# Emptying attention's last blocks in three steps between output matmuls, and moving two zero loads to GpSimd's queue

## The chip, the core and the metric

The kernel runs on one core of one Trainium2 chip. The metric is the device time of one execution in microseconds. The kernel before takes 1247.27 us (median of three runs, 1247.18 to 1247.7).

Engine names: PE is the tensor engine's matmuls, PEld its weight loads, DVE the vector engine, ACT the scalar engine, POOL is GpSimd, SP the sync engine. SPq, ACTq and POOLq are the queues from which those engines issue transfers. PSUM is the memory that takes the results of matmuls. An issue holds its queue (or, on GpSimd, the engine) for the time that the profile shows for it; a transfer lands when its data have arrived.

## The reference, cut to what matters

Two independent parts share one output tensor. Part A is a state space layer of 1024 states over 2048 steps. Part B is attention with memory, in 64 segments of 32 tokens plus 8 memory rows, with 32 heads of 128, followed by an output projection:

```python
for s in range(n_seg):
    xs = x[:, s * seg_len:(s + 1) * seg_len, :].copy()
    h = jnp.concatenate([mem, xs], axis=1)
    q = jnp.einsum('btd,dhe->bhte', h, Wq)      # k and v likewise
    scores = jnp.einsum('bhqe,bhke->bhqk', q, k) * scale
    scores = jnp.where(mask[None, None], scores, -1000000000.0)
    p = _softmax(scores, axis=-1)
    o = jnp.einsum('bhqk,bhke->bhqe', p, v)
    o = jnp.einsum('bhte,hed->btd', o, Wo)
    mem = o[:, :M, :].copy()
    outs.append(o[:, M:, :])
...
return jnp.concatenate([a, b], axis=-1)
```

The kernel computes all segments at once with a guess of the memory rows, checks the guess at the end, and has a slow path.

## The kernel before

The order of the program is: part A with the V projection of part B; then attention, in which head pairs (16 of them, `HP`) are projected to q and k while the pair before goes through scores and softmax; then the output projection. PE is given its work in small steps by Python generators. `proj` yields after each projection group, `attention` after each pair of block groups (11 per head pair, `NU`), `outproj_first` after every four output matmuls.

```python
def load_v(self, hp):
    if hp < HP:
        k = self.k
        vt = self.vts[hp % 2]                    # [128, 22, 272] bf16, two buffers
        if hp < 2:                               # the rows past 99 are zeroed once per buffer
            z = self.vx[0][T + 32:T + 32 + 128 - GW, 0:2 * EW].unsqueeze(1).to_broadcast([128 - GW, NG, 2 * EW])
            k.tc.keep_in_program_order(k.SP.dma_start(vt[GW:128, :, :], z))
        hb, cs = ...
        k.tc.keep_in_program_order(k.SP.dma_start(vt[0:GX, :, :], self.vx[hb].rearrange("(g p) n -> p g n", p=GX)[:, :, cs]))
        k.SP.dma_start(vt[GX:GW, :, :], self.vt[hb].rearrange("(g j) n -> j g n", j=3)[:, :, cs])
        self.vtile[hp] = vt
```

Here `GX` is 96, `GW` is 99 and `NG` is 22. So a zero load writes partitions 99 to 127, that is 29 of them, with 22 rows of 544 bytes each: 638 rows, 347,072 bytes (339 KB of 1024).

```python
def att_front(self, hp, u):
    ...                                          # four scores matmuls into PSUM
    k.S.activation(e[:], s[...], ACT.Exp, ...)   # ACT: exponential
    k.G.tensor_tensor(m[...], e[:], mask[...], ALU.mult)   # POOL: times the mask
    return [(hp, 4 * u + b, m, b) for b in range(4)]       # four pending blocks

def att_back(self, blocks):                      # up to three blocks: values, 1/sum, scale
    ...
    for i, (_, b, m, j) in enumerate(blocks):
        PE.matmul(o[:, i, 0:EV], m[:, j * GP:j * GP + 128], vt[:, b // 2, ...], start=True, stop=True)
    V.reciprocal(r, o[0:GW, 0:n, E])
    V.tensor_tensor(self.ob[:, b0:b0 + n, :], o[...], r..., ALU.mult)
    ...                                          # after the last block: stores of ob

def attention(self):
    pend = []

    def back(keep):
        while len(pend) > keep:
            n = min(3, 2 * NG - pend[0][1])
            self.att_back([pend.pop(0) for _ in range(n)])
    for hp in range(HP):
        for u in range(NU):
            if u == 2:
                self.load_v(hp + 1)
            pend += self.att_front(hp, u)
            back(8)
            yield hp, u
    back(0)
    yield HP, 0
```

The loop that drives it. From the moment that the projections run out (in head pair 15), each yield is followed by one step of the output projection:

```python
for n, (hp, u) in enumerate(at):
    if n == 12:
        k.SP.dma_start(wo0[:], b.Wo[:, :, 0:512])          # 4 MB
    ...
    while done < want:
        next(pr)                                           # projection steps
        done += 1
    if done == 18 * HP:
        ...
        next(first)                                        # four output matmuls
```

Two tiles share memory across the border between part A and attention: one of the two q tiles of attention lies where a buffer of part A's output (`a_ot`) was. Its zeroing on DVE therefore waits until part A's last store has landed.

## Time and profile before

| | before |
|---|---|
| span of the profiled run | 1245.6 us |
| PE busy | 1234.4 us, 99% |
| share of PE in the chain that ended last | 98% |
| PE idle in the stretch 480 to 1000 us | 0 |
| PE waits for the mask product | 0.20, 0.26 and 0.43 us, at 1009 to 1016 us |

The first part of the page of the kernel before (busy time, share of the span, number of instructions):

```profile
span 1245.6 us, 20120 instructions
PE 1234.4 (99%) x8270; PEld 662.3 (53%) x8342; DVE 668.0 (54%) x1250; ACT 263.5 (21%) x631; POOL 275.8 (22%) x407
```

PE is the limit. The list of waits of PE between 1000 us and the end has one line: who waited, for whom, the total, how often, and the longest.

```profile
PE psO L64 <- POOL b_m L644: 0.9, 3, 0.4
```

The timeline of the kernel before, where attention ends (start, length, engine, line, operation; in brackets the idle time of that engine and what ended it):

```profile
1014.21 0.34 PE L64 MATMUL psS<-b_q,b_k 128*128 128x99 bf16 x4
...
1014.55 1.03 PE L64 MATMUL psP<-t,b_wv 128*128 128x512 bf16 x4
...
1015.31 0.87 POOL L644 TENSOR_TENSOR b_m<-b_e,maskB 99x396 bf16<-99x396 bf16 x1 [0.34 <-ACT b_e L641]
1015.42 0.39 PE L64 MATMUL psO<-b_v,b_m 128*128 128x129 bf16 x4
...
1016.24 0.29 PE L64 MATMUL psO<-b_v,b_m 128*128 128x129 bf16 x2 [0.43 <-POOL b_m L644]
1016.37 0.28 PE L64 MATMUL psR<-b_v,b_m 128*128 128x129 bf16 x2
```

The last scores are followed by four output matmuls and then by all eight pending blocks.

GpSimd and DVE, before:

```profile
476.89 0.10 DVE L568 MEMSET b_q<- 128x50 bf16 x1 [0.54 <-DMA out_dram<-a_ot]
...
489.75 0.88 POOL L644 TENSOR_TENSOR b_m<-b_e,maskB 99x396 bf16<-99x396 bf16 x1 [0.92 <-ACT b_e L641]
493.16 0.87 POOL L644 TENSOR_TENSOR b_m<-b_e,maskB 99x396 bf16<-99x396 bf16 x1 [2.54 <-ACT b_e L641]
```

The mask products come every few microseconds, and PE reads the third of them (493.16 us) at 494.37 us.

### The profile page before, as it was taken

The numbers are of one execution on the slowest core, as the hardware profiler recorded it, in microseconds if no ns is written. First come the engines' busy times: TensorE is split into PE (matmuls) and PEld (weight loads), VectorE is DVE, ScalarE is ACT, GpSimd is POOL, SyncE is SP. The second block draws the span as 40 slices with busy tenths as digits, with TensorE's granted clock in tenths as the row PEclk, the third lists the DMA queues.
The fourth block names the chain that finished last, engine by engine and source line by source line (L and its number), as shares of the span: only waits on it lengthen the run. The fifth ranks groups of instructions, "written<-read, shape, count | busy, mean of one in ns | idle before, by whom it ended". The sixth has DMA issues, their size and how long they took to land.

```text
span 1245.6 us, 20120 instructions
## 1 busy us (share of the span) xinstructions
PE 1234.4 (99%) x8270; PEld 662.3 (53%) x8342; DVE 668.0 (54%) x1250; ACT 263.5 (21%) x631; POOL 275.8 (22%) x407
## 2 busy tenths in 40 slices
PE   9999999999999999999999999999999999999998
PEld 5444444444455555556666656555665554446444
DVE  4688899998711124666666666666666641001000
ACT  5344444443310000211112111111211110000000
POOL 4111331212332321322222222222222220000000
PEclk9999999999999999999999999999999999999999
DMA  9965444554898834664454544545473289407000
GB/s 245 272 192 148 131 132 128 144 156 107 241 323 247 251 116 95 192 167 123 95 144 108 144 108 114 138 92 133 96 155 95 61 223 220 110 18 153 17 17 27
DMA packets 316022, 176.83 MB, mean 142 GB/s; under 512 B 138650, under 2 KB 301326, under 8 KB 315926
## 3 DMA queue, kind: packets, MB, share of 16 engines
q1 hardware_dynamic: 293830, 147.95, 48.1%
q10 hardware_dynamic: 21072, 24.38, 5.9%
q0 software_dynamic: 1024, 3.17, 0.7%
q8 instruction: 66, 1.08, 0.4%
q14 instruction: 30, 0.25, 0.1%
HBM read 89.14 MB, written 53.17 MB: 114 GB/s over the span
## 4 chain that ended last, share of the span: by engine, by line
PE 98%; DMA 1%; issue 0%; ACT 0%; POOL 0%; DVE 0%; SPq 0%; ACTq 0%
PE psP L64 82%; PE psU L64 9%; PE psS L64 3%; PE psO L64 2%; PE psR L64 2%; DMA wo<-in_B_Wo_dram 1%; DMA b_xr<-in_B_x_dram 0%; ACT b_xe L89 0%; POOL b_m L644 0%; DVE b_ost L91 0%; SPq L64 0%; ACT b_e L641 0%; ACTq L89 0%
## 5 line engine op out<-in xcount | busy, mean ns | idle before, releaser
L64 PE MATMUL psP<-b_xe,b_wq 128*128 128x480 bf16 (+1 forms) x1280 | 247.7, 343 | 0.1
L64 PE MATMUL psP<-b_xe,b_wk 128*128 128x480 bf16 (+1 forms) x1280 | 247.7, 343 | 0.0
L64 PE MATMUL psP<-b_wv,b_xe 128*128 128x512 bf16 (+2 forms) x1033 | 223.4, 372 | 1.0 <-ACT b_xe L89 0.2
L644 POOL TENSOR_TENSOR b_m<-b_e,maskB 99x396 bf16<-99x396 bf16 x160 | 139.8, 874 | 334.0 <-ACT b_e L641 334.0
L641 ACT ACTIVATE b_e<-psS 99x396 bf16<-99x396 f32 x176 | 88.2, 501 | 532.2 <-PE psS L64 527.9
L64 PEld LDWEIGHTS <-b_wk 128*128 128x128 bf16 x1280 | 119.4, 98 | 94.2
L64 PEld LDWEIGHTS <-b_wq 128*128 128x128 bf16 x1280 | 118.7, 98 | 87.7
L64 PEld LDWEIGHTS <-b_xe 128*128 128x128 bf16 x1056 | 101.8, 98 | 119.1 <-ACT b_xe L89 0.4
L91 DVE CAST b_k<-psP 128x480 bf16<-128x480 f32 (+1 forms) x192 | 97.5, 529 | 101.1 <-PE psP L64 101.1
L91 DVE CAST b_q<-psP 128x480 bf16<-128x480 f32 (+1 forms) x192 | 97.5, 529 | 93.0 <-PE psP L64 91.4
L64 PEld LDWEIGHTS <-b_ol 128*128 128x128 bf16 x864 | 84.3, 98 | 94.4
L64 PE MATMUL psU<-a_xT,a_bt 128*128 128x512 bf16 x493 | 113.9, 379 | 1.1
L64 PE MATMUL psP<-t,a_hl 128*128 128x512 bf16 x496 | 112.1, 379 | 0.8
L91 DVE CAST b_ost<-psP 128x512 bf16<-128x512 f32 (+1 forms) x17 | 11.5, 676 | 183.4 <-PE psP L64 182.4
L64 PE MATMUL psP<-wo,b_ol 128*128 128x512 bf16 (+1 forms) x440 | 91.9, 364 | 0.4
L64 PE MATMUL psP<-t,b_ol 128*128 128x512 bf16 x408 | 91.7, 379 | 0.4
L280 POOL TENSOR_SCALAR a_tt<-a_pr,a_tabf 128x1 f32<-128x1 f32 x48 | 34.1, 709 | 243.5 <-DVE a_pr L275 243.5
L89 ACT ACTIVATE b_vst<-psP 128x512 bf16<-128x512 f32 x126 | 72.0, 589 | 71.0 <-PE psP L64 65.0
L661 DVE TENSOR_TENSOR b_ob<-psO,b_accR 99x384 bf16<-99x384 f32 x160 | 85.9, 553 | 2.0
L267 DVE TENSOR_TENSOR a_pr<-psU,a_tabf 128x2048 f32<-128x2048 f32 x32 | 73.0, 2282 | 15.7 <-PE psU L64 14.0
L64 PEld LDWEIGHTS <-a_bt 128*128 128x128 bf16 x512 | 49.2, 98 | 57.6
L64 PEld LDWEIGHTS <-a_hl 128*128 128x128 bf16 x512 | 49.1, 98 | 56.7
(200 smaller groups left out, 963.8 us busy)
## 6 DMA issues: line engine op xcount, KB each, us to landing
b_v<-b_vx SPq DMA_DIRECT2D x16, 1122.0 KB
b_wv<-in_B_Wv_dram SPq DMA_DIRECT2D x16, 1024.0 KB
b_on<-b_ob SPq DMA_DIRECT2D x15, 960.0 KB
b_vx<-b_vst ACTq DMA_DIRECT2D x24, 544.0 KB
a_hs<-a_h SPq DMA_DIRECT2D x32, 256.0 KB
b_wog<-in_B_Wo_dram SPq DMA_DIRECT2D x4, 2048.0 KB
b_wq<-in_B_Wq_dram SPq DMA_DIRECT2D x16, 512.0 KB
b_wk<-in_B_Wk_dram SPq DMA_DIRECT2D x16, 512.0 KB
```

The lines of the kernel that those rows point to most:

```text
L64: r = f(*a, **kw)
L89: self.S.activation(out, in_, ACT.Copy)
L91: self.V.tensor_copy(out, in_)
L267: V.tensor_tensor(pr[:], u[:].unsqueeze(1).to_broadcast([128, 2, 2, TB]), view(t3, [[TB + 1, 2], [TB + 1, 2], [1, TB]]), ALU.mult)
L280: G.tensor_scalar(tt[:, j:j + 1], w[:, j, TB - 1:TB], t3[:, 1, TB:TB + 1], None, ALU.mult)
L641: k.S.activation(e[:], s[0:GW, :, :, 0:GW], ACT.Exp, scale=float(E) ** -0.5, accum_out=self.accE[0:GW, i:i + 1])
L644: k.G.tensor_tensor(m[0:GW, 0:4 * GP].rearrange("p (a b q) -> p a b q", a=2, b=2)[:, :, :, 0:GW], e[:], mask[0:GW, :, :].unsqueeze(2).to_b ...
L661: V.tensor_tensor(self.ob[:, b0:b0 + n, :], o[0:GW, 0:n, 0:E], r.unsqueeze(2).to_broadcast([GW, n, E]), ALU.mult)
```

## The change

The intent: spare PE the last wait by putting output matmuls between the last three groups of blocks, and take the two zero loads, behind which the sync queue is held for some 16 us each, off that queue. The whole diff:

```diff
@@ load_v
-                k.tc.keep_in_program_order(k.SP.dma_start(vt[GW:128, :, :], z))
+                k.tc.keep_in_program_order(k.G.dma_start(vt[GW:128, :, :], z))
@@ attention
-        back(0)
-        yield HP, 0
+        for keep in (6, 3, 0):
+            back(keep)
+            yield HP, 0
```

## The prediction

> **What bounds the kernel.** The tensor engine. The page's first part has PE busy 1234.4 of 1245.6 us (99%) at full clock; the chain that ended last is 98% PE. In the table of 40 us windows PE is busy 40.00 of 40.00 us in each window from 480 to 1000 us, nearly all of attention. The change removes no matmul, so it can only win idle PE time, 11 us in the whole program, most of it at the start, after the last matmul, and as 0.2 us per window elsewhere.
>
> **Part 1, the emptying.** The list of waits gives PE three waits for the mask product on GpSimd: 0.20, 0.26 and 0.43 us, all between 1009 and 1017 us, where the output projection's steps (four matmuls, 0.86 us) replace the longer projection steps. The timeline shows the last: after the last scores PE does four output matmuls, then all eight pending blocks at once; the fourth and later need the mask product that ends at 1016.18 us, and PE restarts at 1016.24. With three blocks, four output matmuls, three blocks and so on, the second group comes at about 1016.55, after the mask. The 0.43 us goes; the other two waits lie inside the loop and stay. The price: the last block is written some 1.3 us later (two steps less the 0.43), so the stores of b_ob and the transposed loads behind them, issued from 1017.7 and 1024.8 us, move as much. Those transposes are issued by 1042.5 us and first used at 1065.7 us: about 20 us of slack. Worth: -0.4 us.
>
> **Part 2, the zero loads.** Each writes 29 partitions x 22 rows of 544 B (638 rows, 339 KB). The tile view of b_v has a longest issue of 15.9 us on the sync queue, held 16.1 and 17.8 us at 466 and 489 us. The Trainium skill, "DMA: Bandwidth & Descriptors", section "Why a DMA increments its semaphore by 16 and not by 1", says a copy is spread over the largest number of engines up to 16 that divides the outer dimension: 29 gives one; the 15.9 us (21 GB/s, worked out) agree. Moving them frees about 32 us of the sync queue, so weight loads go out some 16 us earlier. But PE waits for none of them there. Worth: 0.
>
> The risk is on GpSimd. The first load falls into its idle stretch (461 to 488 us). The second sits among head pair 0's mask products: the third ends at 494.03 us and is read at 494.37; if the load holds GpSimd from 490.63 us, about 2.7 us fit before PE stalls. GpSimd's issues in this trace took 0.52 to 0.56 us for 8 as for 128 rows, so I estimate under 1 us for 638, and no stall. If its descriptors back up behind one DMA engine as on the sync queue, GpSimd is held about 16 us and PE loses about 13 us (1%), or something between. I give that one chance in five.
>
> **Prediction.** 1247.27 - 0.4 = 1246.9 us; range 1246.0 to 1249.0. Faster by over 2%: 1%; within 2%: 98%; slower by over 2%: 1%.
>
> **What would show it.** Two waits of PE for the mask product left, the 0.43 gone; three groups of psO/psR matmuls with psP matmuls between. No 16 us issues on the sync queue at 466 and 489 us; two zero loads on GpSimd's. PE still 40.00 of 40.00 from 480 us; mask products at 488 to 496 us unmoved.
>
> **What would make it wrong.** A long hold of GpSimd by the second load (PE idle near 494 us); another instruction order from the scheduler; earlier weight loads colliding with output stores at 466 to 480 us.

## More of the kernel before

`vx[0]` has zeros from row T + 32 to its end at T + 64.

The zero loads and the V loads, in the timeline of the sync queue (an entry's length is how long the issues held the queue; each `b_v` entry is a zero load and the V load behind it):

```profile
466.23 16.11 SPq L64 DMA_DIRECT2D b_v<-b_vx  x2
482.39 4.25 SPq L64 DMA_DIRECT2D b_wq<-in_B_Wq_dram  x1
486.68 2.65 SPq L64 DMA_DIRECT2D b_wk<-in_B_Wk_dram  x1
489.43 17.82 SPq L64 DMA_DIRECT2D b_v<-b_vx  x2
```

Narrower windows of the timeline and of the DMA view part the first entry (each issue, then its size):

```profile
466.23 0.32 SPq L64 DMA_DIRECT2D b_v<-b_vx  x1
b_v<-b_vx SPq DMA_DIRECT2D x1, 338.9 KB
466.60 15.74 SPq L64 DMA_DIRECT2D b_v<-b_vx  x1
b_v<-b_vx SPq DMA_DIRECT2D x1, 1122.0 KB
```

The zero load is issued in 0.32 us (the second one in 1.86 us). The long issue, 15.74 us (15.92 us in the second entry), is that of the V load behind it: the zero rows move at 39 to 41 per us until about 482 us, and only then do the V load's rows move, at up to 516 per us.

The zeroing of the q tile waits for part A's last store, which lands just before 476.89 us; nothing stands behind it yet.

## The result, and the profile after

The changed kernel takes 1248.89 us (median of four runs, 1248.05 to 1249.16) against 1247.24 us (four runs, 1247.18 to 1247.7) for the kernel before. The ratio is 1.0011, with a 95% interval of 0.9994 to 1.0029. A ratio here is the mean time of one kernel's fast runs over that of the other's fast runs of the same rounds, so it is not quite the ratio of the medians. By that interval the two are the same; still, each of these four runs of the changed kernel was slower than each of these four of the kernel before (in a later round one run of the kernel before took 1248.38 us). The expected 0.4 us were not gained, about 1.6 us were lost.

The changed kernel's page and its list of waits of PE (the wait for `hpb` is the start of the program, and is there before too):

```profile
span 1246.3 us, 20124 instructions
PE 1234.5 (99%) x8270; PEld 662.3 (53%) x8342; DVE 668.1 (54%) x1250; ACT 263.6 (21%) x631; POOL 283.0 (23%) x409
```

```profile
PE psR L64 <- DVE hpb L105: 1.3, 1, 1.3
PE psR L64 <- POOL b_m L644: 0.7, 1, 0.7
PE psP L64 <- DVE b_q L91: 0.6, 1, 0.6
PE psO L64 <- POOL b_m L644: 0.5, 2, 0.3
```

The 0.43 us wait is gone and the 0.20 and 0.26 us are left, as intended. Two waits are new: 0.7 us for a mask product, and 0.6 us for a copy on DVE. The table of stretches, for the window 480 to 520 us in the kernel before and then in the changed one (length of the stretch, then busy time and instructions of PE, PEld, DVE, ACT, POOL; granted clock; DMA share of 16 engines; GB/s):

```profile
480.00:520.00 40.00, 40.00 (x285) 23.04 (x284) 22.34 (x53) 6.56 (x23) 9.61 (x11) 1.00 0.57 124
```

```profile
480.00:520.00 40.00, 38.67 (x269) 21.97 (x268) 23.67 (x61) 6.51 (x22) 13.24 (x12) 1.00 0.82 172
```

PE lost 1.33 us in this one window, in which it never idled before. The timeline of the changed kernel there:

```profile
460.56 3.73 POOL L624 DMA_DIRECT2D b_v<-b_vx  x1
...
468.23 1.25 SPq L64 DMA_DIRECT2D b_v<-b_vx  x1
469.53 15.15 SPq L64 DMA_DIRECT2D b_wq<-in_B_Wq_dram  x1
...
479.87 0.10 DVE L568 MEMSET b_q<- 128x50 bf16 x1 [3.84 <-DMA out_dram<-a_ot]
...
480.17 0.59 DVE L91 CAST b_q<-psP 128x480 bf16<-128x480 f32 x1
...
480.81 3.40 PE L64 MATMUL psP<-b_xe,b_wq 128*128 128x480 bf16 x16 [0.61 <-DVE b_q L91]
...
491.37 3.68 POOL L624 DMA_DIRECT2D b_v<-b_vx  x1 [0.30 <-PE psP L64]
...
495.07 1.71 POOL L644 TENSOR_TENSOR b_m<-b_e,maskB 99x396 bf16<-99x396 bf16 x2
...
496.01 0.23 PE L64 MATMUL psR<-b_v,b_m 128*128 128x129 bf16 x1 [0.72 <-POOL b_m L644]
```

Two chains can be read off. First, part A's last store now lands at about 479.8 us, 3 us later. On DVE the copy that frees a PSUM buffer (480.17 us) comes behind the zeroing, and PE restarts behind that copy. Second, the zero load among the mask products holds GpSimd for 3.68 us; the third mask product starts at 495.07 in place of 493.16 us, and PE waits for it.

And the place of the emptying, after:

```profile
1016.66 0.87 POOL L644 TENSOR_TENSOR b_m<-b_e,maskB 99x396 bf16<-99x396 bf16 x1 [0.34 <-ACT b_e L641]
1016.77 0.33 PE L64 MATMUL psO<-b_v,b_m 128*128 128x129 bf16 x3
...
1016.94 1.03 PE L64 MATMUL psP<-t,b_wv 128*128 128x512 bf16 x4
...
1017.80 0.33 PE L64 MATMUL psO<-b_v,b_m 128*128 128x129 bf16 x3
```

The second group of blocks starts at 1017.80 us, after the mask product has ended at 1017.53, with no wait.

### A finer ruler: the same matmuls in two traces

The instruction list of PE is nearly the same in all kernels, so the start of one and the same matmul can be compared between traces. Five marks cut the program: P, the first projection of head pair 0; S, the first scores; Q, the first projection of head pair 1; O, the first output matmul; L, the first output matmul with the fourth quarter of the heads. In the kernel before they start at 471.11, 486.84, 501.88, 1006.15 and 1025.98 us. The differences to the kernel before, worked out from the start times in the traces, one profiled run each:

| run | start to P | P to S | S to Q | Q to O | O to L | L to end |
|---|---|---|---|---|---|---|
| changed kernel | -0.32 | **+0.77** | **+0.89** | 0.00 | **-0.61** | 0.00 |

Start to P varies from run to run (-0.03 to -0.52 in the runs below, whatever the kernel). Everything else that isn't touched repeats to 0.2 us, mostly to 0.01 us. So the change is a sum of three terms: -0.61 for the emptying, +0.77 for the late store, +0.89 for the held GpSimd. Together with the start they give +0.73 us, and the profiled run of the changed kernel (1248.05 us, the fastest of its four) was 0.74 us over that of the kernel before (1247.31 us). No ratio of run times has an interval that lies wholly on one side of 1, so what follows rests on these start times, from one profiled run of each kernel.

One thing about the ruler: 0.61 is more than the 0.43 us that the list of waits shows. The idle time in the list begins at the recorded end of the matmul before it, and matmuls are recorded as longer than the pace at which they follow each other: 0.22 us against some 0.06 us for those of the blocks. The Trainium skill, "Perfetto Trace Analysis", section "Tensor Engine Instruction (MATMUL, LD_WEIGHTS)", says that the profiler estimates a matmul's end from its size and does not observe it. The traces agree: three single waits of 0.43, 0.61 and 0.72 us cost 0.61, 0.77 and 0.89 us, each 0.16 to 0.18 us more than listed.

### The profile page after: what moved, and what is told of

Same layout as the page of the kernel before. It is cut to its first block, busy times and chain, and to the rows that moved or that the text cites. A ratio compares the mean times of both kernels' runs of the same rounds, so it can differ in the third digit from the quotient of the medians.

```text
span 1246.3 us, 20124 instructions
## 1 busy us (share of the span) xinstructions
PE 1234.5 (99%) x8270; PEld 662.3 (53%) x8342; DVE 668.1 (54%) x1250; ACT 263.6 (21%) x631; POOL 283.0 (23%) x409
## 4 chain that ended last, share of the span: by engine, by line
PE 97%; issue 1%; DMA 1%; POOL 0%; DVE 0%; another core or an unknown queue 0%; ACT 0%; POOLq 0%; DVEq 0%; ACTq 0%
PE psP L64 81%; PE psU L64 9%; PE psS L64 3%; PE psO L64 2%; PE psR L64 2%; DMA out_dram<-a_ot 1%; POOL b_m L644 0%; POOL b_v L624 0%; ACT b_e L641 0%; DVE a_ot L327 0%; DVE b_xe L91 0%; DVE b_q L91 0%; DVE b_ost L91 0%; DVE a_n L963 0%
## 5 line engine op out<-in xcount | busy, mean ns | idle before, releaser
L267 DVE TENSOR_TENSOR a_pr<-psU,a_tabf 128x2048 f32<-128x2048 f32 x32 | 73.0, 2282 | 15.7 <-PE psU L64 14.0
```

The source lines that it names most:

```text
L267: V.tensor_tensor(pr[:], u[:].unsqueeze(1).to_broadcast([128, 2, 2, TB]), view(t3, [[TB + 1, 2], [TB + 1, 2], [1, TB]]), ALU.mult)
```

## The experiments

Theory A: the emptying wins 0.6 us; each zero load loses something, the first by way of the late store, the second by holding GpSimd. Rival B: the emptying costs more than it wins, because the last stores come later, and the loads cost nothing. Inside A two things were open: what delays the store (the V load of head pair 0, whose rows now move from about 473 in place of about 482 us, or the zero rows' own traffic), and why GpSimd is held so long.

### The parts one by one (four kernels, five rounds)

Only the emptying, the loads as before:

```diff
 # against the changed kernel
-                k.tc.keep_in_program_order(k.G.dma_start(vt[GW:128, :, :], z))
+                k.tc.keep_in_program_order(k.SP.dma_start(vt[GW:128, :, :], z))
```

> Only the emptying in three steps; both zero loads stay on the sync queue. Theory A (the emptying wins about 0.6 us, the moved loads lose about 1.6 us or more): 1246.6 us, 0.4 to 0.7 us under the kernel before; PE waits for the mask product only twice (0.20 and 0.26 us), no PE wait at 480 or 495 us. Rival B (the later stores at the end cost more than the emptying wins, and the loads cost nothing): 1248.5 to 1249 us, as the changed kernel.

Measured: 1246.86 us (1246.17 to 1247.05) against 1247.36 us before (1247.18 to 1248.38), ratio 0.9995. PE's new waits are absent.

Only the loads, the emptying as before:

```diff
 # against the changed kernel
-        for keep in (6, 3, 0):
-            back(keep)
-            yield HP, 0
+        back(0)
+        yield HP, 0
```

> Only the two zero loads on GpSimd's queue; the emptying as before. Theory A: 1249.0 to 1249.8 us, about 0.6 us over the changed kernel, with PE waits of about 0.6 us at 480 us (DVE memset behind the last store of part A) and 0.7 us at 495 us (mask product behind a GpSimd issue of 3.7 us). Rival B: 1247.2 us, as before.

Measured: 1249.22 us (1248.3 to 1249.45), with PE waits of 1.0 us at 481 us and 0.7 us for the mask product.

Three steps, only the first load on GpSimd's queue:

```diff
 # against the changed kernel
-                k.tc.keep_in_program_order(k.G.dma_start(...))
+                k.tc.keep_in_program_order((k.G if hp == 0 else k.SP).dma_start(...))
```

> Three steps, and only the first zero load (head pair 0, GpSimd idle) on GpSimd's queue. Theory A: the wait at 480 us stays (0.5 to 1.5 us), the wait at 495 us is gone: 1247.2 to 1248.2 us. If the hold of GpSimd were the whole loss: 1246.6 us.

Measured: 1247.62 us (1246.97 to 1247.78). The wait behind the late store is there (1.2 us), the one for the mask product isn't.

Three steps, only the second load on GpSimd's queue:

```diff
 # against the changed kernel
-                k.tc.keep_in_program_order(k.G.dma_start(...))
+                k.tc.keep_in_program_order((k.SP if hp == 0 else k.G).dma_start(...))
```

> Three steps, and only the second zero load (among head pair 0's mask products) on GpSimd's queue. Theory A: the wait at 480 us is gone, the one at 495 us stays, with a GpSimd issue of 3.7 us: 1246.6 + 0.9 = 1247.5 us (1247.2 to 1247.8). If the hold of GpSimd cost nothing: 1246.6 us.

Measured: 1247.73 us (1247.34 to 1248.23). The wait behind the store is gone; GpSimd is held 3.73 us again. Here the load could start at 490.40 us, so the loss is a little smaller and falls in several small gaps.

| run | median us | P to S | S to Q | Q to O | O to L |
|---|---|---|---|---|---|
| only three steps | 1246.86 | 0.00 | 0.00 | 0.00 | -0.61 |
| only the loads | 1249.22 | +1.18 | +0.89 | 0.00 | 0.00 |
| steps, first load moved | 1247.62 | +1.36 | 0.00 | 0.00 | -0.61 |
| steps, second load moved | 1247.73 | 0.00 | +0.58 | +0.18 | -0.61 |

Rival B falls: the emptying by itself gives all of its gain, and the stretch from L to the end is unchanged in the traces. Theory A stands: each stretch answers to one part of the change and to no other. The loss behind the store isn't constant (0.77, 1.18, 1.36 us so far); it depends on when a transfer lands.

### What makes the load so expensive (four kernels)

The second load moved ahead of the mask products:

```diff
 # against the changed kernel
-            if hp < 2:
+            if hp == 0:
                 z = ...
-                k.tc.keep_in_program_order(k.G.dma_start(vt[GW:128, :, :], z))
+                for v in self.vts:
+                    k.tc.keep_in_program_order(k.G.dma_start(v[GW:128, :, :], z))
```

> Changed kernel, but both zero loads go to GpSimd's queue one after the other before its first mask product, in its idle stretch of 461 to 488 us. If the hold of the queue (3.7 us) is what costs 0.9 us at 495 us: that wait is gone, the stretch from the first scores to the second head pair's first projection is back at the 15.04 us of before, total 1247.6 us (1247.2 to 1248.2), with the wait at 480 us left. If it is the zero load's traffic among the other transfers that costs it: 1248.5 us or more.

Measured: 1248.26 us (1247.93 to 1248.6). This one missed its aim. The second load did not start in the idle stretch: its issue begins at 488.77 us, although GpSimd had nothing else to do from 464.4 us on. The first load took 27.5 us to land, and 460.72 + 27.5 = 488.2 us lies just ahead of 488.77, so it looks as if the second waited for the first; that was not tested. The hold, now in front of the first mask product, cost +0.74 us from S to Q.

The second load cut in two halves around a mask product:

```diff
 # against the changed kernel
-                k.tc.keep_in_program_order(k.G.dma_start(vt[GW:128, :, :], z))
+                for g in ((slice(0, NG),) if hp == 0 else (slice(0, NG // 2),)):
+                    k.tc.keep_in_program_order(k.G.dma_start(vt[GW:128, g, :], z[:, g, :]))
@@ attention
+                if hp == 0 and u == 3:
+                    ...                          # the second half: groups 11 to 21 of self.vts[1]
                 pend += self.att_front(hp, u)
```

> Changed kernel, with the second zero load cut in two halves of 11 rows a partition (319 rows each), one before head pair 0's third mask product and one before its fourth. If the hold goes with the rows: two issues of about 1.9 us on GpSimd, each inside the 2.7 us of slack, no PE wait near 495 us, 1247.6 to 1248.2 us. If a hold is a fixed 3.7 us for any such load: two waits, 1249.5 us or more.

Measured: 1247.70 us (1247.17 to 1248.32). The halves hold GpSimd for 2.62 and 2.59 us, not 1.9, but still under the 2.7 us of slack: S to Q is +0.00, and the wait for the mask product is gone. P to S is +1.45, since the first load was left as it was. So the slack read from the trace of before was right, and it was the length of the hold that had been mis-sized.

Now the width. 29 partitions is a prime number; 32 is not. The tile's rows 96 to 98 are overwritten afterwards by the load of the three extra rows, so zeroing 96 to 127 gives the same result. On the sync queue, where nothing goes through GpSimd at all:

```diff
 # against the changed kernel
-                z = self.vx[0][T + 32:T + 32 + 128 - GW, 0:2 * EW].unsqueeze(1).to_broadcast([128 - GW, NG, 2 * EW])
-                k.tc.keep_in_program_order(k.G.dma_start(vt[GW:128, :, :], z))
+                z = self.vx[0][T + 32:NSLOT, 0:2 * EW].unsqueeze(1).to_broadcast([128 - GX, NG, 2 * EW])
+                k.tc.keep_in_program_order(k.SP.dma_start(vt[GX:128, :, :], z))
@@ main loop: the scheduler would otherwise move the 4 MB load ahead of these
-                k.SP.dma_start(wo0[:], b.Wo[:, :, 0:512])
+                tc.keep_in_program_order(k.SP.dma_start(wo0[:], b.Wo[:, :, 0:512]))
```

> Three steps; both zero loads on the sync queue as before, but 32 partitions wide (96 to 127) and ahead of the three extra rows, so that they can spread over 16 engines: issue of 1 to 3 us in place of 15.9. The 4 MB output weight load is pinned to its place. Nothing goes through GpSimd's queue. If the wait at 480 us comes from the V load of head pair 0 going out 14 us earlier, ahead of the last store of part A: the wait stays (0.6 to 1.4 us), 1247.4 to 1248.0 us. If it comes from the zero rows' own traffic through GpSimd's queue: no wait, 1246.9 us.

Measured: 1246.71 us (1246.3 to 1246.77), the three steps' gain in full; P to S and S to Q are 0.00. The first zero load and the V load together hold the sync queue for 0.92 us at 465.83 us in place of 16.11. And the V load goes out even earlier than in the changed kernel (its rows move from about 467 us), yet PE does not wait. So the early V load alone is not the cause, and the first of the two answers in the expectation falls.

The same width on GpSimd's queue:

```diff
 # against the run above
-                k.tc.keep_in_program_order(k.SP.dma_start(vt[GX:128, :, :], z))
+                k.tc.keep_in_program_order(k.G.dma_start(vt[GX:128, :, :], z))
```

> One look at the length of GpSimd's issue: zero loads of 32 partitions (704 rows) on GpSimd's queue, the 4 MB load pinned. If the 3.7 us go with the number of rows: about 4.1 us. If they come from all rows going to one engine (29 partitions): 0.6 to 1 us, and the load lands in a few us in place of 27 to 35. A late load of the three extra rows may stop PE near 493 us here, so its time is not to be read.

> The look with 32 partitions on GpSimd's queue again, timed: 1246.7 us (1246.3 to 1247.0), 2.2 us under the changed kernel, the same as three steps alone.

Measured: 1246.66 us in the look (a single run, so its state is unknown), and 1246.66 us (1246.42 to 1246.77) when timed, ratio 0.9994. The feared late load of the extra rows did not stop PE. P to S and S to Q are 0.00 in both. The tile view of `b_v` shows why. In the changed kernel, 29 partitions (duration of an issue in ns, lowest, median and highest; then the time from issue to landing in us):

```profile
L624 POOL DMA_DIRECT2D b_v<-b_vx x2: 3681/3704/3727, 460.6 to 491.4; - x2
...
DMA to landing us min/median/max: 26.7/30.8/34.9
```

In the timed run with 32 partitions:

```profile
L624 POOL DMA_DIRECT2D b_v<-b_vx x2: 737/756/776, 460.9 to 490.5; - x2
...
DMA to landing us min/median/max: 4.3/5.7/7.1
```

More rows (704 for 638), a fifth of the hold, a fifth of the time to land. The transfers show one engine at work. In the kernel before, from 496 to 506 us, while the second zero load drains on the sync queue (packets, MB, share of 16 engines):

```profile
q1 hardware_dynamic: 391, 0.21, 7.4%
```

In the changed kernel, from 516 to 524 us, while it drains on GpSimd's queue (q0) with a load of the sync queue (q1) beside it:

```profile
q0 software_dynamic: 33, 0.14, 5.1%
q1 hardware_dynamic: 32, 0.03, 1.5%
```

One of 16 engines is 6.25%, and these rows move at 21 and 22 GB/s. In the first stretch never more than two of the queue's packets are in flight at once; in the second it is exactly one, on the two queues together, for 96% of the time. (With 32 partitions up to 18 of the load's packets are in flight at once.) In the second stretch the two queues together fill just one engine, and the load on the sync queue, that of wq for head pair 2, probably waits for its own rows on that engine (read from the numbers, not tested): its issue held the queue for 24.94 us (499.31 us in the changed kernel's timeline), as had the one at 469.53 us for 15.15 us. Moving the zero loads did not free the sync queue. It moved the hold from one load behind them to another: before it was the V load that was held, for 15.74 and 15.92 us, now it is that of wq.

The packet sizes in the traces show one thing more. On GpSimd's queue each load of 29 partitions consists of 79 packets of 8 rows and one of 6, and beside them of 15 x 79 packets of 32 bytes and 15 of 24 bytes: as if each of fifteen other engines got a 4-byte entry for every row. The two halves above have them too, the loads of 32 partitions have none. That writing these entries is what holds GpSimd for 3.7 us is likely, but was not tested apart from the width.

A control, since the pinned 4 MB load was a second edit:

```diff
 # against the changed kernel
-                k.SP.dma_start(wo0[:], b.Wo[:, :, 0:512])
+                tc.keep_in_program_order(k.SP.dma_start(wo0[:], b.Wo[:, :, 0:512]))
```

> Control: the changed kernel with nothing but the 4 MB output weight load pinned to its place. If the width of the zero load, and not the pinning, repaired the earlier run: as the changed kernel, 1248.3 to 1249.3 us, GpSimd issues of 3.7 us, PE waits at 480 and 495 us. If the pinning did it: 1246.7 us.

Measured: 1248.46 us (1248.3 to 1248.68; four runs), holds of 3.7 us, P to S +1.11, S to Q +0.90. The pinning repaired nothing; the width did.

What of the store? The start of the zeroing on DVE that waits for it, in the trace of each run:

| zero load of head pair 0 | V load of head pair 0 | zeroing starts at us | after P, us | PE waits |
|---|---|---|---|---|
| 29 partitions, sync queue (before; three steps only; second load moved; deeper emptying below) | late | 476.4 to 476.9 | 5.8 | no |
| 32 partitions, sync queue or GpSimd (the deeper one below too) | early | 478.0 to 478.6 | 7.2 to 7.6 | no |
| 29 partitions, GpSimd (changed; loads only; first load moved; both early; halves; pinned) | early | 479.9 to 480.6 | 9.1 to 9.8 | 0.6 to 1.3 us |

(Late: its rows move from about 482 us. Early: from 467 to 473 us.) The column after P leaves out the varying start, and it gives PE's margin: in each of the six kernels in which PE waits, the loss from P to S is the zeroing's time after P less 8.31 or 8.32 us. So the store may slip by 2.5 us at no cost, and each us beyond that costs one.

Two things together use up this margin, each too small by itself: with loads that go out ahead of the store it slips by 1.4 to 1.8 us, and where zero rows crawl through one engine for some 20 us at the same time it slips by another 1.5 to 2.6 us. (No run has the crawl on GpSimd's queue with a late V load, so that the two simply add is read from the table.) By what path the store is delayed was not separated; the trace doesn't name the engine of a packet. It does rule out that only the store's rows on the busy engine are late. The store is issued 0.92 us after P in all these kernels, and its first packet moves 1.8 us after P where the V load is late, but 4.5 to 5.7 us after P where it is early, wide or narrow; its last packet starts 6.3 to 7.0 us after P with 32 partitions and 8.0 to 8.5 us after P with 29 on GpSimd.

### Does it go further? (two kernels, five rounds)

The two waits that the three steps leave, 0.20 and 0.26 us, come from the same place: steps so short that the mask product of the step before isn't ready. The kernel has five mask buffers and uses three, so one more step may pend:

```diff
 # against the run with only three steps
-                back(8)
+                back(11 if hp == HP - 1 and u > 5 else 8)
-        for keep in (6, 3, 0):
+        for keep in (9, 6, 3, 0):
```

> Zero loads on the sync queue as before; emptying in four steps, and in the last head pair up to 11 blocks may wait from its seventh pair of groups on in place of 8, so that a mask product has one more step of time. PE's two waits left for the mask product (0.20 and 0.26 us) should go: the stretch from the first output matmul to the fourth quarter of its heads 1.07 us under the kernel before in place of 0.61, total 1246.3 us (1245.9 to 1246.7).

Measured: 1245.97 us (1245.83 to 1246.14) against 1247.33 us before (1247.05 to 1247.7), ratio 0.9989. O to L is -1.42, more than the -1.07 expected, because each wait costs its listed time and some 0.17 us: 0.20 + 0.26 + 0.43 + 3 x 0.17 = 1.40. The list of waits of PE in this run has one line left, that of the program's start:

```profile
PE psR L64 <- DVE hpb L105: 1.3, 1, 1.3
```

The same with the zero loads 32 partitions wide on GpSimd's queue and the 4 MB load pinned:

> The same deeper emptying, with the zero loads 32 partitions wide on GpSimd's queue and the 4 MB load pinned. If PE bounds and both causes are repaired, freeing the sync queue still wins nothing: the same 1246.3 us as with the loads on the sync queue (1245.9 to 1246.7), no PE wait at 480 or 495 us.

Measured: 1245.63 us (1245.49 to 1245.76), ratio 0.9986 (95% interval 0.9973 to 1.0000). Each of its runs is faster than each run of the kernel before and of the changed kernel; it is the best, 1.7 us under the one and 3.3 us under the other. From P to the end its trace equals that of the run above to 0.06 us. The 0.34 us between the two medians are thus about the 0.28 us by which P came earlier, a stretch that no edit touches. A free sync queue won nothing that the traces show.

## Why the prediction was right or wrong

The predicted range (1246.0 to 1249.0 us) and "within 2%" held. The predicted direction did not: 0.4 us faster was forecast, some 1.6 us slower was measured. That the range held is luck: no term of the sum leads to 1248.9 us, the median lies 0.11 us inside the upper end, and one of the four runs (1249.16 us) lies outside.

- **What bounds the kernel: right.** PE's busy time is the same to 0.1 us in both pages, and every difference is PE idle time.
- **Part 1, the emptying, "-0.4 us": right in mechanism, off in size.** The wait went, the other two stayed, the later stores cost nothing, as said. (The wait begins with the fifth pending block, not the fourth as written; nothing hangs on it.) It was worth 0.61 us by the traces, because the listed wait of 0.43 us begins at an estimated end.
- **Part 2, "GpSimd's issues took 0.52 to 0.56 us for 8 as for 128 rows, so I estimate under 1 us for 638, and no stall": wrong; this step failed.** The hold was 3.7 us. The trace of before has issues of 0.52 to 0.73 us, and all of them were of loads of another kind: those of 128 rows moved with up to 18 packets in flight at once, the 638 rows with never more than one. The prediction had itself worked out that 29 partitions mean one engine, and named the possibility as the one-in-five risk, but let an estimate from loads of another shape overrule it. The size of the slack (2.7 us) was right: 2.6 us did not stall PE, 3.7 us did.
- **Part 2, "PE waits for none of them there. Worth: 0": wrong.** It is true that PE gained nothing from the free queue, but loads that go out earlier meet other traffic. The collision was named under "what would make it wrong", with the right stretch of time, and not costed: it was worth +0.77 to +1.45 us. The partner in it was also incomplete. Not the early loads alone delayed the store by enough to stop PE, but early loads together with a load crawling on one engine.
- **"Moving them frees about 32 us of the sync queue": wrong.** The prediction took the issues of 15.7 and 15.9 us for those of the zero loads. They were the V loads', held while the zero rows drained; with the zero loads on GpSimd the weight loads of wq were held for 15.15 and 24.94 us instead. The one-engine reading itself was right: 638 rows at some 40 per us are 16 us.

The sum with the measured terms: -0.61 + 0.89 + (0.77 to 1.45) = +1.05 to +1.73 us before the varying start, against a difference of the medians of 1.65 us.

## What to carry to other kernels

A transfer's cost lies in its shape before it lies in its queue: with an awkward partition count, as the prime 29 here, it may run on one engine wherever it is issued, so widen or split it first (29 to 32 partitions made the hold 3.7 to 0.76 us and the landing some 30 to 6 us). A long issue need not be the fault of the transfer that shows it: look at the sizes, and at what was issued just before. A queue that is blocked for 16 us and delays nothing isn't worth unblocking, and what it held back may be better where it was: before moving a transfer, ask which store or load its neighbours will now run into, and what stands in order behind that. When a short idle time of an engine is to be filled, compare the start times of the same instructions in two traces, which here resolved 0.01 us where the run times resolved about 0.5.

## What the Trainium skill lacked or had wrong

- "DMA: Bandwidth & Descriptors", section "Why a DMA increments its semaphore by 16 and not by 1": its rule for the number of engines (the largest up to 16 that divides the outer dimension) fits what was seen on the sync queue: 29 partitions drained at 21 GB/s and 7.4% of 16 engines, with at most two packets in flight. It reports an exception, that some copies issued from GpSimd are spread over 16 engines all the same, with data on as many as the partitions need. This load was none of those: 22 GB/s, and 6.6% of 16 engines together with the load beside it. The page doesn't say which copies get the exception, nor that a load from GpSimd that stays on one engine comes with further small packets (15 x 79 of 32 bytes and 15 of 24 for the 638 rows here).
- The same page, section "Anatomy of one DMA — SWDGE (gpsimd) path", calls the time to generate descriptors small and variable and says that many can be emitted before it shows. Here it showed: 3.7 us for 638 rows of 29 partitions, 2.6 us for 319, but 0.74 to 0.78 us for 704 rows of 32 partitions. A sentence that the partition count decides, and that GpSimd's own work waits meanwhile, is missing there.
- "Perfetto Trace Analysis", section "DMA Instruction — SWDGE (GPSIMD)", says that the recorded end of such an instruction is when the descriptors have been written, not when the data have moved. The runs agree (3.7 us recorded, 26.7 to 34.9 us to landing). It lacks the consequence that a transfer still draining lengthens the issues of loads behind it, on the same queue (15.74 and 15.92 us before the change) and on another (15.15 and 24.94 us after it).
- The same page says that a matmul's end is estimated; it gives no size. Here it hides 0.16 to 0.18 us of each wait of PE.
- "DMA: Bandwidth & Descriptors", section "Issuing engines are not separate DMA queues", was right: another issuing engine only saves issue time. Here it did not even save that.
